# Finished rows written over their summands, and another reckoning in the list planner

## The chip, the cores and the metric

One core of one Trainium2 chip runs the whole program. The metric is the device time of one execution in microseconds (us).

## What is computed

```python
def _attn_ref(q, k, v):                       # (8, 8, 576, 64), chunks of 64
    scores = scale * np.matmul(q_c, k_c.transpose(0, 1, 2, 4, 3))
    scores = scores - np.max(scores, axis=-1, keepdims=True)
    attn = np.exp(scores)
    attn = attn / (np.sum(attn, axis=-1, keepdims=True) + 1e-09)
    out = np.matmul(attn, v_c)
...
def _moe_ref(x, w_in, w_out):                 # x: 4608 x 512, w_in: 512 x 2048, w_out: 2048 x 512
    h = x @ w_in
    g = h * np.cos(h)
    return (g @ w_out).astype(np.float32)
```

Attention within chunks of 64 gives x, 4608 tokens of 512 channels, and two matrix products with an elementwise step between them give the output, 4608 x 512 in float32.

## The kernel before, in words

The tokens are cut into nine tiles of 512. A float32 operand of a product is split into a high and a low part, and a product is three matmuls (high by high, high by low, low by high). The program has these stretches:

- Until about 200 us, tiles 0 and 1, with attention of tiles 0 to 2 and the splitting of the weights. Its order is set by a first list with written due times, which the change doesn't touch.
- From about 200 to 310 us, tile 2. Its first product is taken in a form with seven partial products in place of eight, with sums of blocks of the weights that are made, stored to HBM ("combo" for the first weights, "sums" for the second) and streamed back. The sums for the second weights are made here too, in many small additions.
- From about 310 us, three pairs of tiles (3 and 4, 5 and 6, 7 and 8), each with an **inner** stage (the first product of both tiles, L1952, and the elementwise step with a sine) and an **outer** stage (the second product, L2080), both in the seven-product form. The attention of the next pair of tiles is worked in beside them.

Two tiles of the output are four quarters in an outer stage: C11 and C12 are the left and right half of the columns for the first tile, C21 and C22 for the second. C11 and C12 are copied out of a PSUM bank; C21 is a bank plus u2 (a buffer of the ring w), C22 a bank plus ds (a buffer half0 or half1). Each quarter is worked in two halves. `rows` (L2199) makes such rows in SBUF and a task on SyncE stores them.

A **ring** is a number of SBUF buffers under one name, taken in turn. A task that takes a buffer waits for all users of what was in it. Here the rows of C11 and C21 take buffers of the ring kt (four; otherwise the keys of attention), those of C22 and C12 of the ring g (two). In the inner stage, g holds the two sums of a product, ha and hb (L2053, L2064), of which hb must be there before the last partial product of its pair can be added. The ring vt (two) holds values of attention, loaded at L1470.

From about 200 us on, the order on every engine comes from `planned` (L280). Every piece of work is a task with an engine, a nominal length, its predecessors and, for some, a second engine. The planner runs the list through time, each engine taking the due task that can begin soonest, four times over, and keeps the best. Lengths on engines other than TensorE are multiplied by `WIDER`. Additions with two SBUF operands (marked `port`) may be lent from VectorE to GpSimd by `lent` (L339):

```python
if due[i] + late <= at + SLACK:
    return False
until = at + tasks[i][6][1] + NEXT
return not any(tasks[j][4] and j != i and ready[j] < at + 1.0 and due[j] + late < until for j in can[DVE])
```

`late` is how far TensorE's main work is behind so far. What comes out is a fixed order of instructions for each engine; all DMAs leave from SyncE's queue, in order. Streamed blocks of weights have six rooms.

Of the kernel before, what the change touches and what calls it, by code (L numbers as in the profile page):

```python
# [11 lines left out]
F32 = mybir.dt.float32  # L12
# [6 lines left out]
ALU = mybir.AluOpType  # L19
AX = mybir.AxisListType  # L20

P = 128
TOK = 512
# [36 lines left out]

LOWEST = 7.49 / (1 << 32)

SLACK = 12.0

LOCKED = 9.0

NEXT = 2.0

CARE = 0.8

WIDER = 1.03

ROUNDS = 4

# [2 lines left out]
PE, ACT, DVE, POOL, SP = range(5)  # L77
# [202 lines left out]
def planned(tasks, edges):  # L280
# [40 lines left out]
    def run(due):  # L321
# [17 lines left out]
        def lent(i, e, at):  # L339
            if e == POOL:  # L340
# [4 lines that stand above are left out]
# [9 lines left out]
        for _ in range(n):  # L354
# [24 lines left out]
            if e != PE:  # L379
                length *= WIDER  # L380
            if t:
# [32 lines left out]
def attention_then_cos_ffn(ctx: ExitStack, tc, qT, kT, v, w_in, w_out, out, wide):  # L414
# [5 lines left out]
    NT, HP = qT.shape[0], qT.shape[1]  # L420
# [10 lines left out]
    att = ctx.enter_context(tc.tile_pool(name="att", bufs=2))  # L431
    xp = ctx.enter_context(tc.tile_pool(name="xp", bufs=4))
    gp = ctx.enter_context(tc.tile_pool(name="gp", bufs=3))
# [6 lines left out]
    def kept(ins):  # L440
        tc.keep_in_program_order(ins)
        return ins

    def load(out, in_):
        kept(nc.sync.dma_start(out=out, in_=in_))  # L445
# [4 lines left out]
    def copy_by(by, out, in_):  # L450
        if by == DVE:
            kept(nc.vector.tensor_copy(out, in_))  # L452
        else:
            kept(nc.scalar.copy(out=out, in_=in_))  # L454
# [886 lines left out]
    def room_of(name, bufs=1):  # L1341
        return Room(rings, name, bufs)
# [4 lines left out]
    def task(eng, length, run, *after, new=(), uses=(), lag=None, port=False, table=None, other=None, main=False, at=0.0):  # L1347
        i = len(tasks)
        if lag is None:
            lag = 0.3 if eng == PE else 0.2  # L1350
        tasks.append([eng, length, run, lag, port, table, other, main, at])
        for a in after:
            if a is not None:
                edges.append((a, i, False))
        for r in new:
            edges.append((r.before, i, False))
            if r.last is not None and r.last.first is not None:
                edges.append((r.last.first, i, True))
            r.first = i
            r.users.append(i)  # L1360
        for r in uses:
            if r.first is not None:
                edges.append((r.first, i, True))
            r.users.append(i)
        return i
# [8 lines left out]
    ACT_TOK, DVE_TOK, POOL_TOK = 0.53, 0.6, 1.25  # L1374
# [68 lines left out]
    def both(out, a, b, op):  # L1443
        kept(nc.vector.tensor_tensor(out, a, b, op=op))  # L1444
# [635 lines left out]
    def outer(d):  # L2080
# [4 lines left out]
        st = {}  # L2085
# [112 lines left out]

        def rows(name, half, room, what, *after, add_to=None):  # L2199

            ring, bufs = {"C11": ("kt", HP), "C21": ("kt", HP), "C22": ("g", 2), "C12": ("g", 2)}[name]
            r = room_of(ring, bufs)
            pool = gp if ring == "g" else att

            def go(by=DVE):
                os = st["rows", name, half] = pool.tile([P, TOK], F32, name=ring, bufs=bufs)
                if add_to is None:
                    copy_by(by, os, what())
                else:
                    both(os, what(), add_to[0](), ALU.add)  # L2210
            if add_to is None:
                i = task(ACT, ACT_TOK, go, *after, new=(r,), uses=(room,), other=(DVE, DVE_TOK))
            else:
                i = task(DVE, DVE_TOK, go, *after, new=(r,), uses=(room, add_to[1]))
            done[name, half] = i
            tile_of = ta if name[1] == "1" else tb
            n0 = 0 if name[2] == "1" else HALF
            r0 = tile_of * TOK + 2 * half * P

            def keep():  # L2220
                to = out[r0 : r0 + 2 * P, n0 : n0 + HALF].rearrange("(s p) n -> p s n", s=2)
                load(to, st["rows", name, half].rearrange("p (s n) -> p s n", s=2))
            task(SP, 0.1, keep, i, uses=(r,), lag=2.5)

        def after_phase(ph, half, m):
# [8 lines left out]
            elif ph == 1:  # L2234
                r = rooms["ds", half] = room_of(f"half{half}")

                def keep():
                    st["ds", half] = wts.tile([P, TOK], F32, name=f"half{half}")
                    plain(st["ds", half], st["C", half])
                done["ds", half] = task(ACT, ACT_TOK, keep, m, new=(r,), uses=(rooms["C", half],))  # L2240
            elif ph == 2:
                rows("C11", half, rooms["A", half], lambda: st["A", half], m)
            elif ph == 3:
                r = rooms["u2", half] = room_of("w", 2)

                def keep():
                    st["u2", half] = dec.tile([P, TOK], F32, name="w")
                    plain(st["u2", half], st["B", half])
                done["u2", half] = task(ACT, ACT_TOK, keep, m, new=(r,), uses=(rooms["B", half],))
            elif ph == 4:  # L2250
                rows(
                    "C21", half, rooms["C", half], lambda: st["C", half], m, done["u2", half],
                    add_to=(lambda: st["u2", half], rooms["u2", half]))
            elif ph == 5:
                rows(
                    "C22", half, rooms["B", half], lambda: st["B", half], m, done["ds", half],
                    add_to=(lambda: st["ds", half], rooms["ds", half]))
            else:
                rows("C12", half, rooms["B", half], lambda: st["B", half], m)
# [75 lines left out]
    starts, by = planned(tasks, edges)  # L2335
# [56 lines left out]
```

## Time and profile before

| | us |
|---|---|
| median of 3 runs | 822.25 (818.61 to 824.65) |
| profiled execution, its own time | 820.84 |
| its span, first to last instruction | 819.1 |
| busy TensorE matmul | 796.2 |
| busy VectorE | 705.7 |
| busy ScalarE | 538.8 |
| busy GpSimd | 190.1 |

The engines are PE (TensorE), PEld (its weight loads), DVE (VectorE), ACT (ScalarE), POOL (GpSimd) and SP (SyncE); SPq is SyncE's DMA queue. A name such as g<-h,w_in says which buffers an instruction writes and reads. The span is cut into stretches by stage, and a stretch of time that TensorE isn't busy in is followed back by the timeline, where a bracket gives an engine's idle time just before an instruction and what ended it.

### The profile page before, as it was taken

The numbers are of one execution on the slowest core, as the hardware profiler recorded it, in microseconds if no ns is written. First come the engines' busy times: TensorE is split into PE (matmuls) and PEld (weight loads), VectorE is DVE, ScalarE is ACT, GpSimd is POOL, SyncE is SP. The second block draws the span as 40 slices with busy tenths as digits, with TensorE's granted clock in tenths as the row PEclk, the third lists the DMA queues.
The fourth block names the chain that finished last, engine by engine and source line by source line (L and its number), as shares of the span: only waits on it lengthen the run. The fifth ranks groups of instructions, "written<-read, shape, count | busy, mean of one in ns | idle before, by whom it ended". The sixth has DMA issues, their size and how long they took to land.

```text
span 819.1 us, 17473 instructions
## 1 busy us (share of the span) xinstructions
PE 796.2 (97%) x6720; PEld 701.0 (86%) x6720; DVE 705.7 (86%) x1079; ACT 538.8 (66%) x1014; POOL 190.1 (23%) x165
## 2 busy tenths in 40 slices
PE   6899999999999999999999997999999999999998
PEld 5788888888888878888999996888999988889998
DVE  6899998887889889999999875999999868879853
ACT  4888955455467746777976554898765567665542
POOL 2363764766517251002000100020101000001000
PEclk9999999999999999999999999999999999999999
DMA  9991739495987986975557578655675575555653
GB/s 334 416 413 71 264 123 326 163 325 191 296 276 229 338 279 224 330 247 200 186 201 227 179 250 292 220 194 168 224 229 167 183 236 191 202 180 193 218 182 104
DMA packets 95251, 189.89 MB, mean 232 GB/s; under 512 B 8640, under 2 KB 51648, under 8 KB 95168
## 3 DMA queue, kind: packets, MB, share of 16 engines
q1 hardware_dynamic: 95168, 188.78, 67.6%
q8 instruction: 53, 0.87, 0.4%
q14 instruction: 30, 0.25, 0.1%
HBM read 148.90 MB, written 39.85 MB: 230 GB/s over the span
## 4 chain that ended last, share of the span: by engine, by line
PE 90%; DMA 4%; DVE 3%; issue 1%; SPq 1%; ACT 1%; DVEq 0%
PE acc L448 54%; PE h L448 30%; PE a L448 5%; DMA kt<-in_kT_dram 2%; SPq L445 1%; PE a L1537 1%; DMA qt<-in_qT_dram 1%; DVE w_in L1444 1%; DVE g_lo L458 0%; DMA combo<-w_in 0%; DVE x L458 0%; DMA vt<-in_v_dram 0%; DVE w_in L458 0%; DMA out_dram<-g 0%; DVE g L458 0%
## 5 line engine op out<-in xcount | busy, mean ns | idle before, releaser
L448 PE MATMUL h<-x,w_in 128*128 128x512 f32 (+1 forms) x852 | 190.1, 367 | 0.0
L448 PEld LDWEIGHTS h<-x,w_in 128*128 128x128 f32 x852 | 147.8, 188 | 28.3 <-DVE g L458 0.4
L448 PE MATMUL acc<-w_in,w_in 128*128 128x512 f32 (+1 forms) x702 | 156.5, 349 | 4.6 <-DVE g L1444 4.6
L448 PEld LDWEIGHTS acc<-w_in,w_in 128*128 128x128 f32 x702 | 114.6, 189 | 22.2 <-DVE g L1444 5.1
L448 PE MATMUL acc<-w_out,g_hi 128*128 128x512 f32 x352 | 111.0, 396 | 0.0
L448 PE MATMUL acc<-w_in,g_hi 128*128 128x256 f32 x576 | 104.4, 282 | 0.0
L448 PEld LDWEIGHTS acc<-w_in,g_hi 128*128 128x128 f32 x576 | 88.6, 188 | 0.9
L448 PE MATMUL acc<-x,w_in 128*128 128x512 f32 x276 | 82.1, 390 | 0.0
L448 PE MATMUL acc<-w_in,g_lo 128*128 128x256 f32 x288 | 80.5, 280 | 0.0
L448 PEld LDWEIGHTS acc<-w_out,g_hi 128*128 128x128 f32 x352 | 64.4, 188 | 13.5 <-DVE vt L452 0.3
L454 ACT CAST g_hi<-w_out 128x512 fp32r<-128x512 f32 x83 | 51.5, 621 | 31.2 <-PE acc L448 14.3
L458 DVE TENSOR_TENSOR g_lo<-w_out,g_hi 128x512 fp32r<-128x512 f32 x85 | 61.7, 727 | 10.3 <-ACT g_hi L454 8.6
L448 PE MATMUL acc<-w_out,g_lo 128*128 128x512 f32 x176 | 69.7, 396 | 0.0
L1435 ACT ACTIVATE w_out<-w_out 128x512 f32<-128x512 f32 x96 | 60.1, 632 | 13.1 <-DVE w_out L1431 12.4
L448 PEld LDWEIGHTS acc<-x,w_in 128*128 128x128 f32 x276 | 51.7, 188 | 10.8
L448 PEld LDWEIGHTS acc<-w_in,g_lo 128*128 128x128 f32 x288 | 54.2, 188 | 0.0
L454 ACT CAST g_hi<-g 128x512 fp32r<-128x512 f32 x48 | 29.9, 623 | 24.3 <-DVE g L807 12.3
L1428 ACT ACTIVATE w_out<-g 128x512 int32<-128x512 f32 x48 | 30.2, 631 | 22.6 <-DVE g L1444 21.1
L448 PE MATMUL h<-w_in,g_hi 128*128 128x256 f32 x240 | 43.4, 282 | 0.0
L458 POOL TENSOR_TENSOR w_out<-g,w_out 128x512 f32<-128x512 f32 x5 | 7.5, 1508 | 145.3 <-ACT w_out L1435 145.3
L1431 DVE SCALAR_TENSOR_TENSOR w_out<-w_out,acc 128x512 f32<-128x512 int32 x46 | 31.3, 681 | 11.3 <-ACT w_out L1428 11.0
L458 DVE TENSOR_TENSOR g_lo<-g,g_hi 128x512 fp32r<-128x512 f32 x42 | 37.5, 896 | 2.9 <-ACT g_hi L454 1.9
(209 smaller groups left out, 1678.2 us busy)
## 6 DMA issues: line engine op xcount, KB each, us to landing
w_in<-combo SPq DMA_DIRECT2D x112, 512.0 KB, 4.4
w_in<-sums SPq DMA_DIRECT2D x84, 512.0 KB, 3.6
combo<-w_in SPq DMA_DIRECT2D x56, 256.0 KB, 3.9
sums<-w_out SPq DMA_DIRECT2D x56, 256.0 KB, 4.3
qt<-in_qT_dram SPq DMA_DIRECT2D x36, 256.0 KB, 5.7
kt<-in_kT_dram SPq DMA_DIRECT2D x36, 256.0 KB, 5.8
w_in<-in_w_in_dram SPq DMA_DIRECT2D x16, 512.0 KB, 9.7
w_out<-in_w_out_dram SPq DMA_DIRECT2D x16, 512.0 KB, 9.9
```

The lines of the kernel that those rows point to most:

```text
L445: kept(nc.sync.dma_start(out=out, in_=in_))
L448: kept(nc.tensor.matmul(*args, **kw))
L454: kept(nc.scalar.copy(out=out, in_=in_))
L458: kept(eng.tensor_tensor(out, a, b, op=op))
L1428: kept(nc.scalar.activation(n.bitcast(I32), h, AF.Identity, bias=0.25, scale=0.5 / math.pi))
L1431: kept(nc.vector.scalar_tensor_tensor(g, g.bitcast(I32), -2.0 * math.pi, h, op0=ALU.mult, op1=ALU.add))
L1435: kept(nc.scalar.activation(g, g, AF.Sin, bias=0.5 * math.pi))
L1444: kept(nc.vector.tensor_tensor(out, a, b, op=op))
L1537: kept(nc.tensor.transpose(out=pt[:, i * P : (i + 1) * P], in_=e[:, 2 * i : 2 * i + 2].rearrange("p c k -> p (c k)"), identity=ident,))
```

## The change

C21 and C22 are added in place, over u2 and ds, so that their rows take no buffer of their own. C12 is copied to the ring vt instead of g. C11 stays in kt. Three constants of the planner change: work off TensorE is reckoned 1.08 of its nominal length instead of 1.03; a task may be lent to GpSimd with 6 us to spare instead of 12; and it isn't lent if a `port` task that VectorE could begin is due within 12 us of the lent one's end, instead of 2.

```diff
-SLACK = 12.0
+SLACK = 6.0
...
-NEXT = 2.0
+NEXT = 12.0
...
-WIDER = 1.03
+WIDER = 1.08
...
         def rows(name, half, room, what, *after, add_to=None):
 
-            ring, bufs = {"C11": ("kt", HP), "C21": ("kt", HP), "C22": ("g", 2), "C12": ("g", 2)}[name]
-            r = room_of(ring, bufs)
-            pool = gp if ring == "g" else att
-
-            def go(by=DVE):
-                os = st["rows", name, half] = pool.tile([P, TOK], F32, name=ring, bufs=bufs)
-                if add_to is None:
+            if add_to is None:
+                ring, bufs = {"C11": ("kt", HP), "C12": ("vt", 2)}[name]
+                r = room_of(ring, bufs)
+
+                def go(by):
+                    os = st["rows", name, half] = att.tile([P, TOK], F32, name=ring, bufs=bufs)
                     copy_by(by, os, what())
-                else:
-                    both(os, what(), add_to[0](), ALU.add)
-            if add_to is None:
                 i = task(ACT, ACT_TOK, go, *after, new=(r,), uses=(room,), other=(DVE, DVE_TOK))
             else:
-                i = task(DVE, DVE_TOK, go, *after, new=(r,), uses=(room, add_to[1]))
+                r = add_to[1]
+
+                def go():
+                    os = st["rows", name, half] = add_to[0]()
+                    both(os, what(), os, ALU.add)
+                i = task(DVE, DVE_TOK, go, *after, uses=(room, r))
```

## Rows read from the trace of the kernel before

**Rows 1.** Engine totals: busy us (share of the span) and instructions.

```profile
PE 796.2 (97%) x6720; PEld 701.0 (86%) x6720; DVE 705.7 (86%) x1079; ACT 538.8 (66%) x1014; POOL 190.1 (23%) x165
```

**Rows 2.** Busy us by stage: PE, PEld, DVE, ACT, POOL, granted clock, DMA.

```profile
199.00:216.00 17.00, 15.27 (x87) 13.05 (x86) 12.04 (x24) 8.31 (x21) 9.03 (x11) 1.00 0.74 216
216.00:310.00 94.00, 91.82 (x1021) 79.95 (x1020) 82.65 (x131) 59.05 (x115) 39.82 (x32) 1.00 0.88 290
310.00:400.00 90.00, 90.00 (x583) 74.02 (x582) 86.97 (x139) 69.03 (x128) 9.16 (x8) 1.00 0.70 236
...
487.00:508.00 21.00, 16.36 (x183) 12.81 (x182) 9.48 (x16) 9.39 (x16) 0.00 (x0) 0.92 0.86 287
508.00:570.00 62.00, 62.00 (x391) 50.95 (x390) 59.71 (x97) 54.56 (x106) 6.13 (x5) 1.00 0.61 206
```

**Rows 3.** Timeline at the first seam: start, us, engine, line, operation.

```profile
484.95 0.44 SPq L445 DMA_DIRECT2D out_dram<-kt  x1
...
486.61 1.29 ACT L454 COPY g<-acc 128x512 f32<-128x512 f32 x2
...
491.43 0.33 SPq L445 DMA_DIRECT2D kt<-in_kT_dram  x1
491.87 1.43 SPq L445 DMA_DIRECT2D out_dram<-g  x1
...
494.58 0.39 SPq L445 DMA_DIRECT2D out_dram<-g  x1
...
495.26 1.54 PE L448 MATMUL h<-x,w_in 128*128 128x512 f32 x6
...
495.66 0.69 DVE L1444 TENSOR_TENSOR g<-h,w_in 128x512 f32<-128x512 f32 x1 [3.08 <-DMA out_dram<-g]
...
500.70 0.69 DVE L1444 TENSOR_TENSOR g<-acc,w_in 128x512 f32<-128x512 f32 x1 [3.75 <-issue]
...
501.44 4.60 PE L448 MATMUL acc<-w_in,w_in 128*128 128x512 f32 x12 [4.64 <-DVE g L1444]
```

**Rows 4.** Waits of SyncE's queue, 470 to 510: total us, times, longest.

```profile
SPq L445 <- DMA out_dram<-kt: 5.1, 1, 5.1
```

**Rows 5.** Busy us in two short stretches at the first seam, columns as above.

```profile
496.80:501.40 4.60, 0.00 (x0) 0.00 (x0) 0.85 (x3) 0.22 (x1) 0.00 (x0) 1.00 0.98 373
501.40:506.00 4.60, 4.56 (x16) 3.40 (x16) 4.60 (x8) 3.76 (x7) 0.00 (x0) 0.63 0.82 298
```

**Rows 6.** VectorE's groups by form, 216 to 310: busy us, mean ns.

```profile
L860 DVE TENSOR_TENSOR x<-x,acc 128x512 f32<-128x512 f32 x4 | 2.5, 674 | 0.0
```

**Rows 7.** Timeline of SyncE's queue and of TensorE: loads and use of values.

```profile
462.69 0.83 SPq L445 DMA_DIRECT2D vt<-in_v_dram  x2
...
598.86 1.16 PE L448 MATMUL a<-w_in,vt 64*64 64x64 f32 x64
```

**Rows 8.** Timeline at the second seam, SyncE's queue, VectorE and TensorE.

```profile
663.22 0.39 SPq L445 DMA_DIRECT2D out_dram<-g  x1
...
668.85 0.69 DVE L1444 TENSOR_TENSOR g<-acc,w_in 128x512 f32<-128x512 f32 x1 [2.21 <-DMA out_dram<-g]
...
669.85 2.45 PE L448 MATMUL acc<-w_in,w_in 128*128 128x512 f32 x10
```

**Rows 9.** Timeline of GpSimd, 520 to 545, one row of three.

```profile
537.44 3.56 POOL L458 TENSOR_TENSOR e<-e,z 128x512 f32<-128x512 f32 x3
```

**Rows 10.** Timeline of GpSimd, VectorE and TensorE, 299 to 306.

```profile
299.26 3.52 POOL L458 TENSOR_TENSOR w_out<-half,w_out 128x512 fp32r<-128x512 f32 x2 [6.02 <-ACT w_out L454]
299.30 2.33 DVE L1444 TENSOR_TENSOR w_in<-w_in,e 128x1024 f32<-128x1024 f32 x1
...
301.56 2.30 DVE L458 TENSOR_TENSOR x<-e,w_in 128x1024 fp32r<-128x1024 f32 x1
...
304.91 0.97 PE L448 MATMUL h<-w_in,w_in 128*128 128x256 f32 x6 [1.69 <-DVE w_in L1444]
...
305.97 1.23 DVE L458 TENSOR_TENSOR w_in<-w_in,w_in 128x1024 fp32r<-128x1024 f32 x1 [0.79 <-ACT w_in L454]
```

## The prediction

> **What bounds the kernel now.** I read the engine totals first, then the busy time by stage, then the order of events wherever the busy time of TensorE is below its stretch. TensorE is busy 796.2 of 819.1 us and VectorE 705.7 [rows 1]. By stages [rows 2], TensorE has no gap at all from 310 to 400 and from 508 to 570, the first two inner stages, although VectorE is also nearly full there (86.97 of 90, 59.71 of 62). Gaps lie in three places: 1.73 us in 199 to 216 (17.00 less 15.27), 2.18 us in 216 to 310 (94.00 less 91.82), and 4.64 us in 487 to 508 (21.00 less 16.36). These stretches, with a start that the change doesn't reach, are all that a new order can give back: where TensorE has no gap, its matmuls are the same before and after.
>
> The third place is the seam between the first and the second pair of tiles, and the timeline says how it comes about [rows 3]. Two copies of the last quarter's rows (C12) into the g ring start at 486.61 and take 1.29 together, so the rows are ready at 487.90. Their stores aren't issued then: SyncE's queue is in order, and its head is a load of keys (kt), issued at 491.43, which waits for the store of C21 issued at 484.95, since C21's rows lie in a kt buffer. The queue lost 5.1 us on that one store [rows 4]. The C12 stores leave at 491.87 and 494.58; their landing frees the two g buffers, and only then can VectorE write the two sums of the next pair's first product, at 495.66 (idle 3.08 before it, ended by the store) and at 500.70. TensorE's products need the second sum and start at 501.44 after 4.64 us of nothing. Then they run at a lower granted clock: 0.63 from 501.40 to 506.00, after a stretch without one matmul, where 508 to 570 has 1.00 [rows 2, 5]; 0.63 is a mean of time at 1.2 and at 2.4 GHz. Those 4.60 us held 4.60 x 0.63 = 2.90 us of full-clock work, so 1.70 are lost. The seam costs 4.64 + 1.70 = 6.3 us.
>
> **The change part by part.** *C22 over its summand, C21 over its summand.* The same VectorE additions run, with the output on an operand. The nearest row is an addition of a PSUM bank into the buffer that it reads, 674 ns [rows 6]; the additions into g take 0.69 [rows 3]. Cost nothing, four additions per pair of tiles. No wait is added in front of them, because the wait for a free buffer goes; the buffers half and w are then held until the store has landed, and their next writers come in the next pair's outer stage, over 100 us later. C21 no longer takes a kt buffer, so the load of keys that stood at the head of SyncE's queue loses its 5.1 us wait [rows 4].
>
> *C12 into the vt ring.* The copy is the same. The new wait is that a vt buffer be free of values, and that later values wait for its store. Before, tile 7's values are loaded at 462.69 and first multiplied at 598.86 [rows 7]; in the changed kernel they come in after C12's store, some 35 us later, with 100 us to spare. What is queued behind such a load on SyncE are streamed weight blocks. If the planner sets it too early, the price is a head-of-queue wait like the 5.1 us of [rows 4]; TensorE holds six rooms of blocks, so I take nothing for it and keep the rival below.
>
> *The seam with a free g ring.* The first sum can follow its product. The second needs the product that ends before the h product at 495.26 begins; 495.26 + 0.69 + 0.2 of signalling (an estimate) is 496.15, ahead of 496.80 where that h product ends and TensorE's gap begins [rows 3, 5]. So the next work isn't late: the whole 6.3 us go, unless the new order puts something else there. The second seam gives nothing. There the last store is issued at 663.22, the second sum still waits 2.21 us for its landing, and TensorE goes on at 669.85 without a gap [rows 8].
>
> *The three constants.* They change only the order in which instructions are put on engines after about 200 us, and which VectorE additions go to GpSimd. The planner's lengths of everything but TensorE grow from 1.03 to 1.08 of nominal, so the plan leaves more room. A task may be lent with 6 instead of 12 us to spare, which lends more; but not if a VectorE task of the two-SBUF kind is due within 12 us of the lent one's end instead of 2, which lends less. In the stages where such tasks are always ready I expect the second to win: fewer lent.
>
> What a lent task is worth can be read. One 128x512 addition takes GpSimd 3.56 / 3 = 1.19 us [rows 9] and would take VectorE about 0.69. But while GpSimd works, VectorE's two-SBUF operations stretch: 2.33 and 2.30 instead of 1.23 at 299 to 304, and behind these two TensorE stands still for 1.69 us at 304.91 [rows 10]. The extra 1.10 and 1.07 are each more than the 0.69 that a lent addition saves. The Trainium skill, page "SBUF — State Buffer", section "Who interferes with whom", says that a VectorE instruction with two SBUF inputs and a GpSimd instruction that reads SBUF take a shared port as a lock, and that the loser waits out the whole instruction. The rows agree in kind: by that rule every collision could cost up to a whole GpSimd addition, and fewer lent tasks would be pure gain.
>
> Bounds for the constants, then. Gain: both gaps of the third tile's stage go, 1.73 + 2.18 = 3.9 us [rows 2]. Loss: all that GpSimd did from 216 to 400, 39.82 + 9.16 = 49.0 us, goes back to VectorE at half its time (an estimate from 0.69 against 1.19 to 1.76, the last being 3.52 / 2 [rows 10]), 24.5 us, and no collision is refunded. VectorE's idle time there is 94.00 - 82.65 + 90.00 - 86.97 = 14.4, so 10.1 us are over; the next inner stage adds 6.13 / 2 - 2.29 = 0.8 [rows 2]. Loss at most 10.9. I take a gain of 1.3, a third of 3.9, because the one gap that I can follow back is a collision [rows 10], and a new order may make gaps of its own.
>
> **The sum.** 6.3 + 1.3 = 7.6 us off the profiled execution's 820.84 (span 819.1 and 1.7 around it), which gives 813.2. That execution is 1.4 below the median of the runs, 822.25; against the median the forecast is **814.6**. What this kernel's runs can tell from no change is about 1%, 8.2 us (they reach from 818.61 to 824.65).
>
> **The rivals.** *Both the seam and the collisions go:* 6.3 + 3.9 = 10.2, 812.0. For it: a gap that ends behind stretched additions, and a plan with longer lengths. Against it: the stage has other waits than collisions.
>
> *VectorE becomes the bound (the slower one):* the lent additions come back in the first two inner stages, where VectorE has 3.03 and 2.29 us idle, and in the stage before them. If the bound of 10.9 comes whole, the sum is -6.3 + 10.9 = +4.6: 826.9, slower than before. It decides from the point where more than 6.3 us of VectorE's work can't be placed, that is, where 14.4 + 2.3 + 6.3 = 23.0 of the 27.6 us return without a refund. Against it: refunds, of which two rows alone give 2.17 [rows 10], and copies that may go to ScalarE. The Trainium skill, page "Perfetto Trace Analysis", section "Optimizing Scalar/DVE Operations", speaks on this side: where VectorE is saturated, giving work to GpSimd may make sense, though the shared port may spoil it.
>
> *The seam's wait only moves:* a load (of values for C12's buffer, or of keys) still heads SyncE's queue before a store it needs, blocks come late, and TensorE stands as long as before. Then only the 1.3 is left: 821.0. Against it: the values have over 100 us to spare [rows 7].
>
> **How the numbers follow.** Chances: the forecast 0.50, both go 0.20, the wait moves 0.13, VectorE the bound 0.17. The range runs from 809.5 (812.0, less 2.5 for the spread of the runs around their median) to 823, which leaves out the upper half of the slower rival and little below. Faster by over 1% means under 814.0: all but a little of the second case, and over two fifths of the first (its centre is 0.6 above), 0.42. Slower by over 1% means above 830.5: only the slower rival with an order worse than its bound, and gaps of a new order that I can't see, 0.09. Within 1%: 0.49.
>
> **What would show it.** Right: at the first seam stores of C12 come out of vt buffers, the two sums follow their products without a wait for a store, TensorE has no gap of over 1 us there and the clock stays at 1.00; no load of keys waits for a store of kt for 5 us; GpSimd has fewer instructions after 200 us. The collisions' part: VectorE's 128x1024 additions before 310 at 1.23 throughout and the two gaps smaller. Wrong: gaps of TensorE in 310 to 400 or 508 to 570 ended by VectorE with VectorE at its full time (the slower rival), a long wait in SyncE's queue for a store out of vt (the moved wait), or new gaps in the third tile's stage.

## The result and the profile after

The changed kernel took 812.39 us (median of 4, 812.07 to 813.57) beside 822.02 for the kernel before: ratio 0.9888, interval 0.985 to 0.9926. Run again it took 812.37 (median of 6) beside 821.3: 0.990, interval 0.9884 to 0.9916. It is faster by about 1.0 to 1.1%; forecast were 814.6 and 0.9%.

The page's engine totals of the changed kernel, span 810.4 us:

```profile
PE 794.2 (98%) x6720; PEld 700.1 (86%) x6720; DVE 699.3 (86%) x1087; ACT 533.4 (66%) x1006; POOL 185.9 (23%) x163
```

The stages of the changed kernel, with columns as in [rows 2] (stretch, its length, busy us of PE, PEld, DVE, ACT and POOL, granted clock, DMA):

```profile
199.00:216.00 17.00, 15.60 (x89) 13.31 (x88) 12.95 (x25) 8.76 (x22) 9.53 (x11) 1.00 0.76 229
216.00:310.00 94.00, 93.91 (x1033) 82.38 (x1032) 78.46 (x134) 61.63 (x116) 26.07 (x22) 1.00 0.83 279
310.00:400.00 90.00, 90.00 (x598) 74.75 (x597) 81.97 (x136) 67.30 (x123) 20.11 (x17) 1.00 0.76 255
400.00:487.00 87.00, 86.28 (x976) 84.09 (x975) 82.23 (x126) 55.85 (x125) 0.00 (x0) 1.00 0.64 215
487.00:508.00 21.00, 21.00 (x217) 16.79 (x219) 17.43 (x28) 14.36 (x24) 4.03 (x4) 1.00 0.93 327
508.00:570.00 62.00, 62.00 (x415) 52.02 (x414) 58.73 (x93) 54.89 (x109) 7.64 (x6) 1.00 0.61 206
```

The seam's 4.64 us gap and its clock of 0.92 are gone: 21.00 of 21.00 at 1.00. The third tile's two stretches lose 1.40 and 0.09 where they lost 1.73 and 2.18. One gap of 0.72 us is new, just ahead of the seam. GpSimd isn't used less: 163 instructions, where it had 165. What it did in 216 to 310 (39.82 before, 26.07 now) partly moved to 310 to 400 (9.16 before, 20.11 now).

The timeline of the changed kernel at the first seam, to be laid beside [rows 3]:

```profile
485.75 0.51 SPq L445 DMA_DIRECT2D out_dram<-w  x1
...
486.66 0.97 SPq L445 DMA_DIRECT2D out_dram<-vt  x2
...
488.96 0.69 DVE L1444 TENSOR_TENSOR g<-h,w_in 128x512 f32<-128x512 f32 x1
...
491.65 0.69 DVE L1444 TENSOR_TENSOR g<-acc,w_in 128x512 f32<-128x512 f32 x1 [0.29 <-PE acc L448]
491.73 1.02 SPq L445 DMA_DIRECT2D vt<-in_v_dram  x2
...
492.81 1.52 PE L448 MATMUL h<-x,w_in 128*128 128x512 f32 x6
...
494.17 2.88 PE L448 MATMUL acc<-w_in,w_in 128*128 128x512 f32 x12
```

Both sums now wait for nothing but their products; 12 matmuls take 2.88 us, not 4.60. The new wait is there too: values are loaded into vt at 491.73, behind C12's store, which cost SyncE's queue 2.9 us (its waits from 470 to 512):

```profile
SPq L445 <- DMA out_dram<-vt: 2.9, 2, 2.6
```

TensorE didn't feel it.

**A better ruler.** The program is the same in all kernels until about 200 us. Yet the first half-width product of the third tile, the first that the planner places, starts at another time in each execution. The timeline of TensorE, the kernel before and then the rows alone (below):

```profile
204.30 1.60 PE L448 MATMUL h<-x,w_in 128*128 128x256 f32 x12
```

```profile
202.41 1.60 PE L448 MATMUL h<-x,w_in 128*128 128x256 f32 x12
```

In 14 executions that start lay between 202.41 and 205.63, and the span moves with it. So, for each kernel's profiled execution, I take the span less this start as the time of the planned part. The changed kernel, profiled twice, had 810.4 - 203.99 = 606.4 and 809.1 - 202.77 = 606.3; the kernel before had 819.1 - 204.30 = 614.8. The change is worth 8.4 us there. That is one execution of each kernel, and only the changed one was profiled twice. But TensorE's gaps after the start and the time lost to a lowered clock account for the differences: what is left of the planned part without them lies between 599.9 and 601.0 us in all 14 executions.

### The profile page after: what moved, and what is told of

Same layout as the page of the kernel before. It is cut to its first block, busy times and chain, and to the rows that moved or that the text cites. A ratio compares the mean times of both kernels' runs of the same rounds, so it can differ in the third digit from the quotient of the medians.

```text
span 810.4 us, 17511 instructions
## 1 busy us (share of the span) xinstructions
PE 794.2 (98%) x6720; PEld 700.1 (86%) x6720; DVE 699.3 (86%) x1087; ACT 533.4 (66%) x1006; POOL 185.9 (23%) x163
## 4 chain that ended last, share of the span: by engine, by line
PE 95%; DMA 2%; DVE 2%; issue 1%; ACT 0%; SPq 0%; DVEq 0%
PE acc L448 57%; PE h L448 32%; PE a L448 6%; DMA kt<-in_kT_dram 1%; PE a L1537 1%; DMA qt<-in_qT_dram 1%; DVE w_in L1444 0%; DVE w_in L458 0%; DVE w L458 0%; DVE half L458 0%; PE a L703 0%; DVE x L458 0%; ACT w_in L1561 0%; PE h L703 0%; DVE m L642 0%
## 5 line engine op out<-in xcount | busy, mean ns | idle before, releaser
L448 PE MATMUL acc<-w_in,w_in 128*128 128x512 f32 (+1 forms) x702 | 153.9, 346 | 0.0
L454 ACT CAST g_hi<-w_out 128x512 fp32r<-128x512 f32 x77 | 47.5, 620 | 30.3 <-PE acc L448 14.8
L458 DVE TENSOR_TENSOR g_lo<-w_out,g_hi 128x512 fp32r<-128x512 f32 x80 | 55.6, 696 | 11.6 <-ACT g_hi L454 9.7
L448 PEld LDWEIGHTS acc<-w_out,g_lo 128*128 128x128 f32 x176 | 33.0, 188 | 7.6
L458 DVE TENSOR_TENSOR w_out<-acc,w_out 128x512 f32<-128x512 f32 x46 | 31.5, 685 | 7.9 <-ACT w_out L1435 7.9
L448 PE MATMUL acc<-w_in,pts 128*128 128x256 f32 x288 | 38.2, 281 | 0.0
```

What stands on the lines that cost most here:

```text
L448: kept(nc.tensor.matmul(*args, **kw))
L458: kept(eng.tensor_tensor(out, a, b, op=op))
```

## The experiments

All runs in one table. Each ratio is to the kernel before as run beside that kernel (its medians were 820.5 to 822.02). "Planned part" is the span less the start named above; "gap" is 115 less TensorE's busy us from 195 to 310, and GpSimd its busy us in the same stretch.

| kernel | median us | ratio (95%) | planned part | gap 195 to 310 | GpSimd |
|---|---|---|---|---|---|
| before | 822.02 | | 614.8 | 3.91 | 52.78 |
| changed | 812.39 | 0.9888 (0.985 to 0.9926) | 606.4 | 1.49 | 39.52 |
| changed, again (e12) | 812.37 | 0.990 (0.9884 to 0.9916) | 606.3 | 1.49 | 37.96 |
| e1 rows only | 813.78 | 0.992 (0.9902 to 0.9937) | 608.2 | 4.02 | 50.97 |
| e2 constants only | 816.42 | 0.9946 (0.9926 to 0.9965) | 607.7 | 1.50 | 40.46 |
| e3 C21 in place only | 816.83 | 0.9948 (0.9932 to 0.9965) | 609.5 | 5.41 | 54.85 |
| e10 C12 and C22 moved, C21 in kt | 816.32 | 0.9941 (0.9921 to 0.996) | 609.6 | 5.38 | 55.05 |
| e8 changed, C12 back in g | 817.09 | 0.9946 (0.9928 to 0.9963) | 612.4 | 1.50 | 38.05 |
| e5 rows, WIDER alone | 815.92 | 0.9932 (0.992 to 0.9944) | 608.8 | 2.41 | 54.62 |
| e6 rows, NEXT alone | 812.4 | 0.9895 (0.9882 to 0.9907) | 606.6 | 2.78 | 46.19 |
| e7 rows, SLACK alone | 815.6 | 0.9945 (0.9926 to 0.9964) | 610.3 | 5.93 | 58.45 |
| e4 changed, nothing lent | 815.46 | 0.9933 (0.9917 to 0.9949) | 611.1 | 0.06 | 5.40 |
| e9 changed, nothing lent early | 811.41 | 0.9886 (0.9867 to 0.9904) | 604.7 | 0.06 | 5.54 |
| e11 rows, NEXT, nothing lent early | 812.18 | 0.9894 (0.9876 to 0.9911) | 606.1 | 1.26 | 6.65 |

**Rows and constants apart (e1, e2).** e1 is the changed kernel with the constants of before; e2 is the kernel before with

```diff
-SLACK = 12.0
+SLACK = 6.0
-NEXT = 2.0
+NEXT = 12.0
-WIDER = 1.03
+WIDER = 1.08
```

Expected of e1: 

> The in-place quarters and C12 in vt, with the three constants of before. My theory (the seam comes from where the rows lie): the gap of 4.64 us and the low clock at 487 to 508 go, the third tile's stage keeps gaps of about 3.9 us; 6.3 us off, ratio 0.992. Rival (the reckoning of the list does it, the rows nothing): within 1 us of before, a gap of over 3 us at the seam.

Expected of e2: 

> The three constants alone, rows in kt and g as before. My theory: the seam's gap stays, though its size may shift by 2 us with another order, the third tile's stage gets tidier: 2 to 3 us off, ratio 0.997. Rival (the reckoning does it): the seam closes here too and 8 to 9 us are off, ratio 0.989.

The rows alone take 614.8 - 608.2 = 6.6 us off the planned part, and the third tile's gaps stay as they were (4.02). That is my theory to the letter. The constants alone were expected to leave the seam's gap; they don't. Two lines of e2's list of TensorE's waits (who waited for whom, total us, times, longest), of which the first is the gap left in the third tile:

```profile
PE h L448 <- DVE w_in L1444: 1.4, 1, 1.4
PE acc L448 <- DVE g L1444: 1.2, 1, 1.2
```

The 1.2 is a sum into g again, but at the second seam, where the kernel before had no gap. At the first seam the new order sets C12's stores ahead of the load of keys:

```profile
486.86 0.90 SPq L445 DMA_DIRECT2D out_dram<-g  x2
...
491.50 0.43 SPq L445 DMA_DIRECT2D kt<-in_kT_dram  x1
```

So the rival was half right: either part closes the first seam, and their gains (6.6 and 7.1) don't add up to more than 8.4. By the medians e1 is 2.6 us ahead of e2, by the planned part 0.5 behind; that difference is of the size of the start's spread (202.41 in e1, 205.33 in e2), so I don't rank the two.

**Which row counts (e3, e10, e8).** e3 is the kernel before with C21 alone in place; e10 has the constants of before, C22 in place, C12 in vt and C21 still in a key buffer; e8 is the changed kernel with C12 back in g:

```diff
-            ring, bufs = {"C11": ("kt", HP), "C21": ("kt", HP), "C22": ("g", 2), "C12": ("g", 2)}[name]
+e3:  C21 in place over u2,  {"C11": ("kt", HP), "C22": ("g", 2), "C12": ("g", 2)}
+e10: C22 in place over ds,  {"C11": ("kt", HP), "C21": ("kt", HP), "C12": ("vt", 2)}
+e8:  C21 and C22 in place,  {"C11": ("kt", HP), "C12": ("g", 2)}
```

Expected of e3: 

> The kernel before with C21 alone added in place: no row of C21 in a kt buffer, C22 and C12 still in g. If the seam's wait came from the load of keys that stood in SyncE's queue behind C21's store, the stores of C12 leave some 4 us earlier and most of the 6.3 us go, ratio 0.993 to 0.995, as at the second seam, where g is used by C12 without a gap. If the g ring itself is what costs, the gap stays at over 3 us, ratio 0.998 or more.

Expected of e10: 

> The constants of before, C22 in place and C12 in vt, but C21's rows still in the key buffers. If the free g ring is enough by itself: a load of keys still waits some 5 us for C21's store in SyncE's queue, and TensorE has no gap at the first seam, ratio 0.992 as with all rows moved. If the queue's wait is what costs: a gap of 2 us or more at the seam through late blocks, ratio 0.995 or more.

Expected of e8: 

> The changed kernel with C12 in the g ring as before, C21 and C22 in place, the new constants. If C21 out of the key buffers is all that the seams need: within 0.7 us of the changed kernel, no gap of TensorE at either seam. If the g ring must also be free: a gap of 1 to 2 us at the second seam, ended by a sum into g that waited for a store, and as much over the changed kernel, ratio 0.990 to 0.992.

In e3, with g still used by C12, the seam is closed. VectorE's first sum there waits for its product and not for a store, and TensorE goes from one product to the next (21.00 of 21.00 us busy in 487 to 508):

```profile
496.78 0.69 DVE L1444 TENSOR_TENSOR g<-h,w_in 128x512 f32<-128x512 f32 x1 [1.71 <-PE acc L448]
...
497.99 0.68 DVE L1444 TENSOR_TENSOR g<-acc,w_in 128x512 f32<-128x512 f32 x1
```

In e10 SyncE's queue still waits for stores of kt rows (its waits from 470 to 512; the longest is 3.2 us where the kernel before had 5.1), and TensorE has no gap:

```profile
SPq L445 <- DMA out_dram<-kt: 4.6, 2, 3.2
```

```profile
486.25 0.33 SPq L445 DMA_DIRECT2D kt<-in_kT_dram  x1
...
489.16 1.29 ACT L454 COPY vt<-acc 128x512 f32<-128x512 f32 x2
...
490.77 0.90 SPq L445 DMA_DIRECT2D out_dram<-vt  x2
...
497.81 1.53 PE L448 MATMUL h<-x,w_in 128*128 128x512 f32 x6
499.18 2.91 PE L448 MATMUL acc<-w_in,w_in 128*128 128x512 f32 x12
```

But in e10's order the load of keys that waited is issued at 486.25, before C12's rows are ready at 490.45, and their stores leave 0.3 us after that. So e10 has no late store of C12, and it doesn't test what such a store does to a free g ring. That the stall of the kernel before took a late store is shown by e3; that it took the g ring as well is read from its timeline, where the first sum waits for a store out of g [rows 3], and no run has the late store with g free. By ratio e3 came out as expected, and e10 (0.9941) between its two cases. e3 and e10 come out 1.3 us above e1 in the planned part because their order gave the third tile larger gaps (5.41 and 5.38 for 4.02), not because of the seam.

With the new constants it isn't enough to take C21 out of kt. e8's waits of TensorE for sums into g, and its second seam on the timeline:

```profile
PE acc L448 <- DVE g L1444: 3.8, 2, 2.2
```

```profile
655.35 1.08 SPq L445 DMA_DIRECT2D out_dram<-g  x2
...
661.96 0.69 DVE L1444 TENSOR_TENSOR g<-h,w_in 128x512 f32<-128x512 f32 x1 [3.92 <-DMA out_dram<-g]
...
664.40 4.79 PE L448 MATMUL acc<-w_in,w_in 128*128 128x512 f32 x13 [2.23 <-DVE g L1444]
```

Nothing delays these stores in the queue. The landing alone, until 6.6 us after the issue, is longer than the work that this order has ahead of the sums. The first seam stalls as well, for 1.57 us, again behind sums into g, the first of which waited 4.46 us for a store. e8 loses 612.4 - 606.4 = 6.0 us of the 8.4, where 1 to 2 were expected: 1.57 and 2.23 of gaps, and about 1.8 by the clock (0.94 in 660 to 690). With C12 back in vt, as in the changed kernel, all of it is gone, so here the g ring is shown to be the cause. My reading of the second seam, that it had nothing to give, holds for the order of before alone.

**Which constant counts (e5, e6, e7).** The rows of the change with one constant each (WIDER 1.08; NEXT 12; SLACK 6).

Expected of e5: 

> The new rows with the wider lengths alone (1.08), the old rule of lending. My theory, that the third tile's gaps are collisions with lent additions: the two gaps of about 1.7 us each stay, since as much is lent as before; within 1 us of the rows alone (813.8), ratio 0.992. Rival, that longer lengths in the plan give VectorE room and so close them: both gaps under 0.5 us and 3 us off the rows alone, ratio 0.988.

Expected of e6: 

> The new rows with the stricter rule against lending alone (12 us to the next due task). My theory: fewer lent additions at 200 to 310 (some 30 instead of 40), half the stretching of VectorE, at least the gap at about 301 gone; 1.5 to 3 us off the rows alone, ratio 0.989. Rival (wider lengths do it): the gaps stay, within 1 us of the rows alone.

Expected of e7: 

> The new rows with the laxer rule alone (6 us to spare instead of 12). My theory: more lent, more stretched additions, the gaps at 200 to 310 as large or larger: 0 to 2 us over the rows alone, ratio 0.992 to 0.994. Rival (lent work relieves VectorE where it is full): 1 us or more off the rows alone.

Against the rows alone (608.2): the stricter rule -1.6, the wider lengths +0.6, the laxer rule +2.1. Together they are -1.8, so the stricter rule alone has what there is to have, within what can be told. Each is a difference of single executions. Expected were -1.5 to -3, within 1, and 0 to 2, and the runs keep to that but for 0.1; e5's two gaps of 1.42 and 0.94 lie between its two cases, though (1.7 each, and under 0.5). The gap goes with what GpSimd does beside VectorE: 5.93 at 58.45 us of GpSimd, 4.02 at 50.97, 2.78 at 46.19. The wider lengths break that row: 54.62 us of GpSimd and a gap of 2.41, perhaps because the plan left more room, and what they won there they lost later. In e5's list of TensorE's waits the first line below is what is left in the third tile; the others, with one of 0.3, are waits in later stages:

```profile
PE h L448 <- DVE w_in L1444: 2.4, 2, 1.4
...
PE h L448 <- DVE x L458: 0.7, 1, 0.7
PE acc L448 <- DVE g_lo L458: 0.5, 1, 0.5
```

**What lending is worth (e4, e9, e11).** e4 is the changed kernel with nothing lent in the planned part. e9 has nothing lent in the first 105 us of the planner's time, that is, in the third tile's stretch; e11 is the same on e6's constants.

```diff
-                if due[i] + late <= at + SLACK:
+e4:              (always)
+e9, e11:         if at < 105.0 or due[i] + late <= at + SLACK:
                     return False
```

Expected of e4: 

> The changed kernel with no task lent to GpSimd after about 200 us. My theory (a lent addition saves about what its collisions cost, and VectorE has just room for all): within 3 us of the changed kernel either way, VectorE without a stretched addition, its share in the first two inner stages 97 to 99 of 100. The slower rival of the prediction (VectorE becomes the bound): 5 to 11 us over the changed kernel, gaps of TensorE in 310 to 400 or 508 to 570 that VectorE ends.

Expected of e9: 

> The changed kernel with nothing lent to GpSimd until 105 us of the planner's time, which is the stretch of the third tile. If the gaps left there (1.57 us at 211.5) are collisions: gone, as in the kernel without lending, the outer stages as in the changed kernel, 1 to 2 us off it, ratio 0.987. If VectorE needs the help there: later stages start with more of its work and gaps come at 310 to 480, at or over the changed kernel.

Expected of e11: 

> The new rows, the stricter rule against lending (12 us), the two other constants of before, and nothing lent in the third tile's stretch. By the runs so far: the stage of the third tile as without lending (3 us better than with the stricter rule alone), the later stages as with that rule: 809.5 to 811, ratio 0.986. Rival: a new order of the later stages gives it back, 812 or more.

In e4 the third tile's gaps are gone (0.06 us left), and in e9 too, so lending there is shown to be their cause. How it makes them is seen at the gap of 1.40 us that the changed kernel has left. VectorE's two additions w<-w_out take 2.36 us while GpSimd works on lent ones, and the operand that TensorE waits for comes after them. The changed kernel, then e9, where VectorE does the same additions in the same order and nothing is lent:

```profile
209.29 3.91 POOL L458 TENSOR_TENSOR w_in<-half,w_in 128x256 fp32r<-128x256 f32 x4 [3.95 <-ACT w_in L926]
...
210.25 2.36 DVE L458 TENSOR_TENSOR w<-w_out 128x512 f32<-128x512 f32 x2
...
212.53 0.74 DVE L1444 TENSOR_TENSOR w_in<-h,w_in 128x256 f32<-128x256 f32 x2
...
213.33 0.97 PE L448 MATMUL h<-w_in,w_in 128*128 128x256 f32 x6 [1.40 <-DVE w_in L1444]
```

```profile
209.05 1.29 DVE L458 TENSOR_TENSOR w<-w_out 128x512 f32<-128x512 f32 x2
...
210.25 0.75 DVE L1444 TENSOR_TENSOR w_in<-h,w_in 128x256 f32<-128x256 f32 x2
...
211.06 0.98 PE L448 MATMUL h<-w_in,w_in 128*128 128x256 f32 x6
```

In the kernel before the same pair takes 2.37 us ahead of its gap of 1.73. So both of its large gaps in this stage stood behind stretched additions.

But e4's planned part is 4.7 us longer than the changed kernel's, where my theory had 3 at most. That isn't where the slower rival had put it. The first two inner stages take all the work back without a gap, VectorE with room to spare, 94 and 92% of the time and not the 97 to 99% expected (e4's stages):

```profile
310.00:400.00 90.00, 90.00 (x608) 75.20 (x607) 84.45 (x143) 64.57 (x109) 0.00 (x0) 1.00 0.77 269
508.00:570.00 62.00, 62.00 (x357) 52.15 (x356) 56.82 (x96) 48.80 (x89) 0.00 (x0) 1.00 0.59 203
```

The largest new gap lies in an outer stage, where attention ends: at 454.61 VectorE runs six transposes in a row, 4.28 us, and a low part that TensorE needs comes after them (e4's timeline, then two short stretches of it):

```profile
454.61 4.28 DVE L1531 STREAM_TRANSPOSE w_in<-e 32x512 f32<-32x512 f32 x6
...
458.91 0.69 DVE L457 TENSOR_TENSOR g_lo<-w_out,g_hi 128x512 fp32r<-128x512 f32 x1
...
459.66 0.39 PE L447 MATMUL acc<-w_in,g_lo 128*128 128x256 f32 x1 [2.60 <-DVE g_lo L457]
```

```profile
457.00:460.00 3.00, 0.40 (x3) 0.34 (x3) 2.91 (x5) 1.26 (x2) 0.00 (x0) 1.00 0.36 91
460.00:464.00 4.00, 4.00 (x68) 3.78 (x70) 3.92 (x9) 1.24 (x2) 0.00 (x0) 0.57 0.50 166
```

The stretch after the gap runs at 0.57 of the clock, which costs 1.7 of its 4 us. In all, the outer stages lose 3.95 us more by gaps than in the changed kernel (3.32 for 0.72 in 400 to 487, 1.35 for none in 570 to 660) and 1.7 by the clock, and the third tile gives back 1.4: 4.2 of the 4.7. e9, which lends as the changed kernel does but not beside the third tile, has the gain without this loss: 604.7, which is 1.6 to 1.7 us under the two profiles of the changed kernel. Its median, 811.41, wasn't taken beside the changed kernel's, and the intervals of the two ratios overlap; so what shows e9 ahead is the profile of one execution. It is 1.1% below the kernel before. e11 came out at 812.18, over its expected 809.5 to 811: its order left gaps of its own in the third tile (1.26) and after it (0.53 in 310 to 400) though almost nothing was lent up to 310. So collisions aren't all that makes gaps there.

**The changed kernel once more.** Expected: 

> The changed kernel once more, for an interval as narrow as the other runs have. If all three constants together are worth more than the stricter rule alone (ratio 0.9895 there): 0.987 or less. If the stricter rule is what pays: 0.988 to 0.9905, not to be told apart from it.

 It came out at 0.990, not to be told apart from the stricter rule alone.

## Why the prediction was right

- *The seam.* 6.3 us were forecast from 4.64 of gap and 1.70 of lowered clock. The rows alone gave 6.6. What the prediction didn't have is that the constants close the first seam by themselves (e2): which part is credited with the 6.6 depends on the order in which they are taken. Of the chain that was read from the timeline (C21's store, the load of keys behind it, C12's stores behind that, the g ring), e3 shows the first links: with C21 out of kt the stall is gone. For the last one, the bracket of the second sum at 500.70 names "issue" and not a store [rows 3]. But the three stores of rows from 484 to 503 landed after these times (the view of out_dram):

```profile
DMA to landing us min/median/max: 3.7/6.0/6.5
```

  6.5 fits the load of keys at 491.43 and 3.7 the first sum at 495.66, which leaves 6.0 for the store issued at 494.58: it landed at 500.6, just ahead of the second sum, so the reading holds. That sums into g can stall for stores is shown by e8 in another order; e10 adds only that without rows in g there was no stall.
- *The in-place additions cost nothing*: they wait for no buffer, and take 0.68 to 0.69 as before. *C12 in vt* costs SyncE's queue 2.9 us and TensorE nothing; the rival that the wait only moves didn't come.
- *The constants.* 1.3 us were forecast between a gain of 3.9 and a loss of 10.9; the planned part shows 8.4 - 6.6 = 1.8. The gain came from collisions, as argued: at GpSimd's 5.54 us (e9) the gaps are 0.06, and the one of 1.40 that is left is a collision too. Expected was less lending altogether. That was wrong: 163 instructions for 165, of which ten moved out of 216 to 310. So was that stretched additions would be gone throughout: of the 128x1024 ones two are left in the changed kernel, 1.51 and 2.32 us (VectorE's groups by form, 216 to 310):

```profile
L1444 DVE TENSOR_TENSOR e<-w_in,e 128x1024 f32<-128x1024 f32 x1 | 2.3, 2319 | 0.0
L1444 DVE TENSOR_TENSOR w_in<-w_in,w_in 128x1024 f32<-128x1024 f32 x1 | 1.5, 1512 | 0.4 <-ACT w_in L1561 0.4
```

  TensorE waited behind neither; it did behind the smaller ones at 210.25 (the timeline of the changed kernel beside e9's, above). In e9 all 128x1024 ones take 1.21 to 1.22. The Trainium skill says in "SBUF — State Buffer", section "Who interferes with whom", that the port which these additions share with GpSimd is an exclusive lock. The trace agrees in kind: 2.32 less 1.22 is 1.10, nearly a whole GpSimd addition of 1.19.
- *The slower rival* was right that VectorE can't take everything back, and wrong in place and size: with nothing lent (e4) 4.7 us were lost on balance, all in outer stages, not 10.9 in the inner ones. The Trainium skill says in "Perfetto Trace Analysis", section "Optimizing Scalar/DVE Operations", that giving work of a saturated VectorE to GpSimd may make sense, and that between these two it might not help. The runs agree with both halves: without lending e4 is 6.4 us longer than e9, which lends after the third tile, and lending beside the third tile cost 1.6 to 1.7.
- *The sum.* 7.6 forecast, 8.4 in the planned part. The seam came out a few tenths over its term. The third tile's gaps shrank from 3.91 to 1.49, by 2.4 us where 1.3 was taken as a third of what there was: that term was a choice and not worked out, and it was too small. A new gap takes back 0.72. By the medians 9.6 us are off, which puts the kernel (812.4) beside the rival that both go (812.0) and below the forecast. That nearness is luck: the planned part shows only 8.4 of it, and the third tile still has 1.49 of its gaps. The line of the new gap in the changed kernel's list of TensorE's waits:

```profile
PE h L448 <- DVE x L458: 0.7, 1, 0.7
```

What stays open: why e5's wider lengths cost what they do later. Gaps of 1.5 us there take back nearly all of the 1.6 won in the third tile; why the new order makes them, and where its other 0.8 us go, no run takes apart.

## What to carry to other kernels

A stall at a seam between stages is best read backwards through the in-order DMA queue: what waited there was not the buffer's owner but a load that stood at the head for another store. Taking away the store that the load waited for closed this stall under one order of work (e3); under another order sums waited for the buffers again (e8), so free the buffer of the critical product first. Don't lend additions to GpSimd in a stretch where the critical engine waits for VectorE's two-operand additions: there a lent addition stretches the very engine that it was to relieve. In the later stages lending paid here (e9 beside e4); what makes a stretch fit for it wasn't tested.

## What the hardware showed that was not expected

The same instructions up to 200 us ended 3.2 us apart in 14 executions (202.41 to 205.63). Part of it is the clock: five of the starts, among them the four latest (205.33 to 205.63), had a granted clock of 0.91 from 10 to 30 us, which is 1.8 us of that stretch, and the others 1.00. The spread is more than most of the effects here, and comparing spans from a common instruction on brought two profiles of one kernel to within 0.1 us (606.4, 606.3) where their spans differ by 1.3.

A short gap of TensorE was followed by a low granted clock in two more places: after 2.60 us (0.57 in the next 4 us, e4 above) and after 2.23 in e8, whose stretch of 664.20 to 668.60 had 0.67:

```profile
664.20:668.60 4.40, 4.20 (x13) 3.31 (x14) 4.40 (x8) 2.49 (x4) 1.28 (x1) 0.67 0.33 113
```

Gaps of 1.69 [rows 10] and 1.40 us left it at 1.00 by their stage's rows, and so did one of 2.19 in e7 (1.00 in 306 to 310 behind it).
